# A linear-attention, soft-MoE and MLP kernel: r multiplies, diagonals and one bonus on other engines, w2 rows in long runs, one weight piece narrowed later

## The chip, the core and the metric

The kernel runs on one core of a Trainium2 chip. The metric is device time in microseconds, lower is better; three runs of the kernel before gave 387.38, 387.45 and 388.14 us. The core has TensorE (PE, matmuls), VectorE (DVE), ScalarE (ACT) and GpSimd (POOL), each of which works through its own instructions in the order in which they are written, and SyncE (SP), which issues the loads and stores here.

## The reference, cut

```
# attention: 4 batches, 8 heads, 768 positions, head width 48
for t in range(S):
    cur = einsum('bhd,bhe->bhde', u * k[t], v[t])
    y[t] = einsum('bhd,bhde->bhe', r[t], state + cur)
    state = w[:, :, None] * state + einsum('bhd,bhe->bhde', k[t], v[t])
x = y as 3072 tokens x 384
# first mlp: soft mixture, 8 experts x 4 slots, hidden 1024
logits = x @ phi
slot_input = softmax(logits over tokens).T @ x
slot_out[e] = relu(slot_input[e] @ w1[e]) @ w2[e]
x = softmax(logits over slots) @ slot_out
# second mlp: hidden 2048
h = x @ w_in
out = maximum(0.01 * h, h) @ w_out
```

All arrays are float32.

## The kernel before, in words

**Attention.** The sequence is cut into 6 chunks of 128 positions and the heads into 4 pairs: 24 units, unit i being chunk i // 4 and pair i % 4. The loop over i (line 572) is one turn; in turn i the engines work on units i - 1 to i + 4. For a unit j it runs: `load(j)` in turn j - 4 (rk is r and k by head row, tk is v, k and r by position); `scale(j)` in turn j - 2, which multiplies r and k (two multiplies, lines 305 to 310) by powers of the decay. The k one is always on DVE, the r one on POOL unless j is in `SCALE_V`. Then `bonus(j)` (POOL, lines 316 and 319: r times u, times k), `diag(j)` (DVE sums it into Dg, line 324, and base(j) is filled with the diagonals: eight ACT activations, line 339, or one POOL affine select, line 330, for units in `AFFINE`), and `keys(j)` (line 351, POOL, or DVE for units in `KEYS_V`), all in turn j - 2. In turn j - 1 come `scores(j)` (16 matmuls into A, line 362; the pool of A has one buffer) and `keep(j)` (two predicated copies on DVE from A into base, line 370). In turn j come `attend(j)` (lines 393 and 401, into Y), the copy of Y into xT (line 434), and `update(j)`, the state products U (line 415) and their addition to St on DVE (line 423). The powers of the decay for a head pair are made by `powers` on DVE and ACT, then transposed (line 297) and copied by ACT to KH (line 298), which `keys` multiplies by. U, the transposes psE and px and the tile `low` of the narrowing share a PSUM pool of two buffers. `FILL_L` puts two filling matmuls (line 584) in turn 2. In the second turn of each chunk (i % 4 = 1, "slot turn") the soft-max part of the chunk before is added: transposes, slot products (line 519), acc and sst on DVE (lines 530, 532); its maxima are taken in the turn before (lines 475 to 479).

The weights of both mlps arrive during this: list entry n of `WST` is the turn in which weight load n is issued on SP. The second mlp's weights come as 64-bit numbers and are narrowed to 32 bits: in the turns of `NARROW` three DVE instructions (lines 174, 180, 185) do half a piece, after an ACT instruction (line 170) in a turn of `NARROW_A`.

**First mlp.** `hidden(0)`, `hidden(1)` (line 755) make the slots' hidden values, `outer` (line 798) multiplies by w2: the first half of the experts from tiles loaded by `load_w2`, the second half from `load_rows(f)`, one tile for each of 8 blocks f. Loads of w_out (`load_wout(j)`, tiles wor) are issued among them. Two pieces of w_out are narrowed (`conv_a` on ACT, `conv_b`, `conv_c`, `conv_d` on DVE, lines 848 to 858) and split by `parts` into a high part (woh, ACT, line 864) and a low part (wol, POOL, line 865) around the last `outer`.

**Second mlp.** 96 steps over (token block, hidden block f): a matmul h (line 963), the leaky maximum (t, lines 969 and 973), split into gh and gl (lines 977, 982), and nine products o (line 1020). The products of step n and the preparation of step n + 3 are written in one turn, followed by the jobs listed for n: `job(n, fn, arg)` puts further narrowing there. Steps 4 and 5 are the first with f = 2.

Of the kernel before, what the change touches and what calls it, by code (L numbers as in the profile page):

```python
# [21 lines left out]
NU = NC * NP  # L22
DM = H * D
# [10 lines left out]
NLAST = 3  # L34
NLD = 5
NWT = 18
AFFINE = (0, 1)
KEYS_V = (4, 5, 6)
FILL = {0: 2, 1: 1}
FILL_L = {3: 2}  # L40
WST = [*range(2, 19), 20, 20, 21, 21, NU]
NARROW = [5, 7, 9, 11, 15, 19, 20, 22]
NARROW_A = {3: 5, 6: 7, 7: 9, 10: 11, 14: 15, 18: 19, 19: 20, 21: 22}
SCALE_V = (9, 13, 17, 21)
WCH = 8
WH = WCH // 2
WCW = 768
# [3 lines left out]


def body(
    tc, rk, tok, wT, urep, phi, w1, w2, win, wout, seq, uw, wT1, urep1, rk1, tok1, outT, dbg=None
):
    nc = tc.nc
    ok = chunked(tc, rk, tok, wT, urep, phi, w1, w2, win, wout, outT, dbg, True)


    with tc.If(ok != R * NP):  # L60
        rk2 = nc.dram_tensor("rk2", rk.shape, F32, kind="Internal").ap()
        tok2 = nc.dram_tensor("tok2", tok.shape, F32, kind="Internal").ap()
        general(tc, seq, uw, rk1, tok1, rk2, tok2)
        chunked(tc, rk2, tok2, wT1, urep1, phi, w1, w2, win, wout, outT)


@with_exitstack
# [49 lines left out]


@with_exitstack
def chunked(ctx, tc, rk, tok, wT, urep, phi, w1, w2, win, wout, outT, dbg=None, check=False):  # L120
    nc = tc.nc
    cp = ctx.enter_context(tc.tile_pool(name="cp", bufs=1))
    wp = ctx.enter_context(tc.tile_pool(name="wp", bufs=NWT))
# [220 lines left out]
    def keys(i, eng=nc.gpsimd):  # L344
        if i >= NU - NP:
            return
        hp = i % NP
        kk = tk_t[i][:, 1]
        if i in KEYS_V:
            eng = nc.vector  # L350
        eng.tensor_tensor(
            kk, kk, KH[:, hp : hp + 1, :].broadcast_to([128, B, 2 * D]), op=ALU.mult
        )
# [194 lines left out]

    def load_rows(f):
        t = wp.tile([128, 4, DM], F32, name=f"w2_{f}", tag="wt")  # L550
        nc.sync.dma_start(t, w2[4:, :, f].rearrange("e p d -> p e d"))
        for g in range(4):
            w2_sb[FT * (4 + g) + f] = t[:, g]

# [10 lines left out]
    keep(0)  # L565
    bonus(1, nc.vector)
    diag(1)
    keys(0)
    powers(2)
    powers(3)  # L570

    for i in range(NU):
        c, k = divmod(i, NP)
        for n in range(len(WST)):
            if WST[n] == i:
                load_weights(n)
        if i + NLD - 1 < NU:
            load(i + NLD - 1)
        else:
            load_w2_unit(i + NLD - 1 - NU)  # L580
        if i + 2 < NU:
            scale(i + 2)
        for _ in range(FILL_L.get(i + 1, 0)):
            nc.tensor.matmul(
                lw[0].rearrange("p a t -> p (a t)")[:, C:], ident,
                u_sb.rearrange("p a d -> p (a d)"), start=False, stop=True, skip_group_check=True,
            )
        if i + 1 < NU:
            scores(i + 1)
            keep(i + 1)  # L590
        slot = bool(c) and k == 1
        if i >= 1 and not slot:
            logits(i - 1)
        if 2 <= i < NP:
            tokens(i - 2)(nc.scalar.copy)
        if i + 2 < NU:
            bonus(i + 2, nc.gpsimd if i else nc.vector)
        attend(i)
        if slot:
            soft2(c - 1)  # L600
        evac(i)
        if c and k == 0:
            soft1(c - 1)
        if i < NP - 1:
            powers_t(i + 1)
            keys(i + 1)
        if i == NP:
            nc.gpsimd.memset(ones, 1.0)
        if i == NU - 2:
            yps[NU - 1] = psE.tile([128, 4, C], F32, name="ylast", tag="E")  # L610
            nc.vector.memset(yps[NU - 1][32:64, 0:2], 0.0)
        if check and i == NU - 2:
            rc0 = ap.tile([R, NP], F32, name="rc0")
            nc.vector.tensor_single_scalar(rc0, w_sb, WLO, op=ALU.is_ge)
            nc.vector.scalar_tensor_tensor(rc0, w_sb, WHI, rc0, op0=ALU.is_le, op1=ALU.mult)
            nc.vector.tensor_reduce(mst[:R, 6:7], rc0, op=ALU.add, axis=AX.X)
            nc.vector.memset(mst[:R, 7:8], 1.0)
        if i + 2 < NU:
            diag(i + 2)
            if i + 2 >= NP:  # L620
                keys(i + 2)
        update(i)
        if i >= NP - 1:
            tok_copy = tokens(i - 1)
        if slot:
            pS = slots(c - 1)
            logits(i - 1)
        if i >= NP - 1:
            tok_copy(nc.scalar.copy)
        if slot:  # L630
            slots_add(c - 1, pS)
        if i in NARROW:
            j, x = divmod(NARROW.index(i), 2)
            w = slice(x * WCW // 2, (x + 1) * WCW // 2)
            low = psM.tile([128, WCW // 2], I32, name=f"low{i}", tag="m")
            narrow_b(wirs[j], w, low)
            narrow_c(wi[:, j, w], wirs[j], w, low)
            narrow_d(wi[:, j, w], wirs[j], w, low)
        if i in NARROW_A:
            j, x = divmod(NARROW.index(NARROW_A[i]), 2)  # L640
            w = slice(x * WCW // 2, (x + 1) * WCW // 2)
            narrow_a(wi[:, j, w], wirs[j], w)
# [164 lines left out]
        load_wide(wout[j], wor[j])  # L807

    hs0 = hidden(0)
    for j in range(2):  # L810
        load_wout(j)
    for f in range(2, FT):
        load_rows(f)
    mix(0)
    hs1 = hidden(1, lambda: hidden_t(0, hs0))
    for j in range(2, WH):
# [48 lines left out]
        nc.gpsimd.tensor_tensor(l, w, a.bitcast(F32), op=ALU.subtract)  # L865

    conv_a(0)
    conv_a(1)
    outer(1, range(FT))
    for p in range(2):  # L870
        conv_b(p)
        conv_c(p)
        conv_d(p)
        parts(p)
    for j in range(WH, WCH):
        wirs[j] = wp.tile([128, WCW, 2], I32, name=f"wir{j}", tag="wt")
        load_wide(win[j], wirs[j])
# [183 lines left out]
        job(32 + q, lambda q: late.update({q: spread(1, (2 * q, 2 * q + 1), pH, "h")}), q)  # L1061
        job(32 + q, lambda q: late[q](nc.scalar.copy), q)

    for f in (2, 3):
        job(0, parts, f)

    hid_a(2)
    hid_b(2)
# [54 lines left out]
def _layout(i):  # L1123
    import numpy as np

    r, k, v = (np.asarray(i[n]) for n in ("r", "k", "v"))

    def pad(x):
        y = np.zeros(x.shape[:1] + (2, 64) + x.shape[3:], np.float32)
        y[:, :, :D] = x  # L1130
        return y.reshape(x.shape[:1] + (128,) + x.shape[3:])

    def rows(x):
        y = x.reshape(B, NP, 2, NC, C, D).transpose(3, 1, 2, 5, 0, 4)
# [12 lines left out]
    a["wT"] = wt.reshape(NP, 128)[:, :R].T
    a["urep"] = np.broadcast_to(np.asarray(i["u"]).reshape(NP, 2 * D), (128, NP, 2 * D))
    ph = np.zeros((NP, 2, 64, NS), np.float32)
    ph[:, :, :D] = np.asarray(i["moe_phi"]).reshape(NP, 2, D, NS)  # L1150
    ph = np.stack([ph, ph[:, ::-1]], 1).reshape(NP, 2, 128, NS)
    a["phi"] = ph[:, :, :R].transpose(2, 0, 1, 3)
    a["w1"] = np.asarray(i["moe_w1"]).reshape(E, KT, 128, 2, FE // 2).transpose(0, 3, 2, 1, 4)
    a["w2"] = np.asarray(i["moe_w2"]).reshape(E, FT, 128, DM).transpose(0, 2, 1, 3)
    wi, wo = np.asarray(i["moe2_w_in"]), np.asarray(i["moe2_w_out"])
    wi = wi.reshape(KT, 128, WCH, FF // WCH).transpose(2, 1, 0, 3).reshape(WCH, 128, WCW)
    wo = wo.reshape(WCH, 2, 128, DM).transpose(0, 2, 1, 3).reshape(WCH, 128, WCW)
    s = np.stack([np.asarray(i[n]).reshape(B * H, S, D) for n in "rkv"])
    w, u = (np.asarray(i[n]) for n in "wu")
    uw = np.broadcast_to(np.stack([u, w], 1), (16, H, 2, D)).reshape(128, 2, D)  # L1160

    one = np.zeros((3, D), np.float32)
    one[:, 0], one[:, 1] = (1.0, 0.5, 1.0), (1.0, -0.5, -1.0)
    rk1 = np.broadcast_to(one[:2].T[None, None, :, :, None, None], (1, 2, D, 2, B, C))
    rk1 = pad(rk1)[0]
    tok1 = np.broadcast_to(np.tile(one[1::-1], (1, 2 * B)), (128, 2, 2 * B * D))
    rest = {"win": None, "wout": None, "seq": s, "uw": uw}
    rest["wT1"] = np.ones((R, NP), np.float32)
    rest["urep1"] = np.broadcast_to(np.tile(one[2], 2), (128, NP, 2 * D))
    rest["rk1"], rest["tok1"] = rk1, tok1  # L1170
# [24 lines left out]
```

## Time and profile before

| | |
|---|---|
| median of three runs | 387.45 us |
| profiled execution, whole time | 386.47 us |
| its span, first to last instruction | 384.70 us |
| busy: PE, DVE, ACT, POOL | 367.6, 275.9, 233.3, 144.1 us |
| attention | 0 to about 118 us |
| first mlp | about 123 to 149 us |
| second mlp | about 156 to 380 us |
| DMA, until about 155 us | 16 engines busy nearly all the time, some 410 GB/s |

TensorE is granted full clock throughout (0.999 on average). A timeline row gives start, length, engine, line, operation, output and inputs, shapes, and in brackets how long the engine was idle before it and what ended that. The chain of waits that ended last goes through POOL's products between 22 and 45 us, through TensorE, DVE and ACT in turn from there to 118, and through TensorE's o products at the end.

### The profile page before, as it was taken

The numbers are of one execution on the slowest core, as the hardware profiler recorded it, in microseconds if no ns is written. First come the engines' busy times: TensorE is split into PE (matmuls) and PEld (weight loads), VectorE is DVE, ScalarE is ACT, GpSimd is POOL, SyncE is SP. The second block draws the span as 40 slices with busy tenths as digits, with TensorE's granted clock in tenths as the row PEclk, the third lists the DMA queues.
The fourth block names the chain that finished last, engine by engine and source line by source line (L and its number), as shares of the span: only waits on it lengthen the run. The fifth ranks groups of instructions, "written<-read, shape, count | busy, mean of one in ns | idle before, by whom it ended". The sixth has DMA issues, their size and how long they took to land.

```text
span 384.7 us, 8325 instructions
## 1 busy us (share of the span) xinstructions
PE 367.6 (96%) x3162; PEld 283.4 (74%) x3162; DVE 275.9 (72%) x478; ACT 233.3 (61%) x542; POOL 144.1 (37%) x144
## 2 busy tenths in 40 slices
PE   6889998999999999899999999999999999999994
PEld 3567777787875345788888878888888888888883
DVE  6978888888887448677577746777766766586762
ACT  3288797888894224766765657667655445545440
POOL 4779999977713103336333312554200000000000
PEclk9999999999999999999999999999999999999999
DMA  7999999999999999200022220000000220030202
GB/s 262 401 412 412 407 417 415 418 414 415 399 412 382 371 402 425 84 2 0 0 85 82 83 83 0 1 2 1 2 2 0 82 83 0 1 133 33 82 3 89
DMA packets 21090, 70.16 MB, mean 182 GB/s; under 512 B 2240, under 2 KB 7344, under 8 KB 20912
## 3 DMA queue, kind: packets, MB, share of 16 engines
q1 hardware_dynamic: 21040, 69.53, 46.0%
q8 instruction: 27, 0.44, 0.5%
q14 instruction: 23, 0.19, 0.1%
HBM read 64.80 MB, written 4.72 MB: 181 GB/s over the span
## 4 chain that ended last, share of the span: by engine, by line
PE 76%; DVE 8%; ACT 5%; POOL 5%; issue 2%; DMA 2%; SPq 1%; POOLq 0%; DVEq 0%; ACTq 0%
PE o L1020 51%; PE h L963 6%; ACT base L339 3%; PE po L798 3%; PE ph L755 3%; PE A L362 2%; PE Y L401 2%; DVE base L370 2%; DMA tk<-in_tok_dram 2%; POOL tk L316 1%; POOL rkb L310 1%; POOL tk L319 1%; PE Y L393 1%; PE px L451 1%; DVE Dg L324 1%
## 5 line engine op out<-in xcount | busy, mean ns | idle before, releaser
L977 ACT CAST gh<-t 128x512 fp32r<-128x512 f32 x94 | 58.5, 622 | 69.5 <-DVE t L973 66.6
L973 DVE TENSOR_TENSOR t<-t,h 128x512 f32<-128x512 f32 (+1 forms) x97 | 65.8, 679 | 25.3 <-ACT t L969 24.6
L1020 PE MATMUL o<-gh,wol 128*128 128x512 f32 x279 | 80.2, 393 | 0.0
L1020 PE MATMUL o<-gh,woh 128*128 128x512 f32 x279 | 80.0, 393 | 0.0
L1020 PE MATMUL o<-gl,woh 128*128 128x512 f32 x279 | 79.7, 392 | 0.0
L982 DVE TENSOR_TENSOR gl<-t,gh 128x512 fp32r<-128x512 f32 x71 | 50.2, 707 | 40.4 <-ACT gh L977 40.4
L969 ACT ACTIVATE t<-h 128x512 f32<-128x512 f32 (+1 forms) x97 | 57.4, 592 | 12.5 <-PE h L963 11.2
L1020 PEld LDWEIGHTS o<-gh,woh 128*128 128x128 f32 x279 | 52.4, 188 | 11.8 <-DVE sum L1091 0.2
L1020 PEld LDWEIGHTS o<-gl,woh 128*128 128x128 f32 x279 | 52.5, 188 | 11.7
L1020 PEld LDWEIGHTS o<-gh,wol 128*128 128x128 f32 x279 | 52.2, 188 | 11.7 <-issue 0.4
L339 ACT ACTIVATE base<-anti,Dg 128x128 f32<-128x128 f32 x176 | 53.9, 389 | 10.5 <-DVE Dg L324 9.7
L982 POOL TENSOR_TENSOR gl<-t,gh 128x512 fp32r<-128x512 f32 x23 | 34.3, 1491 | 51.0 <-ACT gh L977 43.6
L370 DVE COPY_PREDICATED base<-mask,A 128x512 f32<-128x512 int32 x48 | 34.2, 734 | 7.4 <-ACT base L339 6.7
L963 PE MATMUL h<-cT,Gs 128*128 128x512 f32 (+1 forms) x97 | 37.4, 391 | 1.4 <-ACT Gs L931 1.4
L362 PE MATMUL A<-rkb 48*128 48x128 f32 x384 | 28.5, 289 | 4.3 <-DVE base L370 2.1
L362 PEld LDWEIGHTS A<-rkb 48*128 48x128 f32 x384 | 24.2, 192 | 9.9 <-issue 3.3
L401 PE MATMUL Y<-base,tk 128*48 128x128 f32 x376 | 25.5, 277 | 0.0
L310 POOL TENSOR_TENSOR rkb<-rkb,ETw 112x512 f32<-112x512 f32 x19 | 23.4, 1234 | 1.9 <-DMA rkb<-in_rk_dram 1.9
L316 POOL TENSOR_TENSOR tk<-tk,u_sb 128x384 f32<-128x384 f32 x21 | 22.1, 1051 | 5.4 <-DMA tk<-in_tok_dram 3.5
L401 PEld LDWEIGHTS Y<-base,tk 128*48 128x48 f32 x376 | 19.4, 122 | 4.9 <-issue 4.3
L963 PEld LDWEIGHTS h<-cT,Gs 128*128 128x128 f32 x97 | 18.0, 188 | 5.6 <-ACT Gs L931 1.8
L865 POOL TENSOR_TENSOR wol<-wor,woh 128x384 fp32r<-128x384 f32 x8 | 9.5, 1198 | 33.3 <-ACT woh L864 33.3
(199 smaller groups left out, 484.0 us busy)
## 6 DMA issues: line engine op xcount, KB each, us to landing
w<-in_w_dram SPq DMA_DIRECT2D x24, 768.0 KB, 8.7
tk<-in_tok_dram SPq DMA_DIRECT2D x23, 576.0 KB, 7.0
rkb<-in_rk_dram SPq DMA_DIRECT2D x24, 512.0 KB, 7.4
wir<-in_win_dram SPq DMA_DIRECT2D x8, 768.0 KB, 11.3
out_dram<-sum SPq DMA_DIRECT2D x17, 256.0 KB, 2.1
wor<-in_wout_dram SPq DMA_DIRECT2D x4, 768.0 KB, 10.3
wir<-in_wout_dram SPq DMA_DIRECT2D x4, 768.0 KB, 4.3
w2t<-in_w_dram SPq DMA_DIRECT2D x4, 576.0 KB, 7.5
```

The source lines that it names most:

```text
L310: (nc.vector if x or i in SCALE_V else eng).tensor_tensor(t, t, e, op=ALU.mult)
L316: eng.tensor_tensor(rr, rr, u_sb[:, hp : hp + 1, :].broadcast_to([128, B, 2 * D]), op=ALU.mult)
L339: nc.scalar.activation(base[i][:, h, b, :], anti, AF.Copy, scale=Dg[i][:, h * B + b : h * B + b + 1])
L362: nc.tensor.matmul(a[:, h, b, :], rk_t[i][p0 : p0 + D, 1, b, :], rk_t[i][p0 : p0 + D, 0, b, :], start=True, stop=True,)
L370: nc.vector.copy_predicated(base[i][:, :, 2 * j : 2 * j + 2, :], mask.unsqueeze(1).unsqueeze(1).broadcast_to([128, 2, 2, C]), a[:, :, 2 * ...
L401: nc.tensor.matmul(ys[r][g : g + D, j, :], v[:, b, D * h : D * h + D], base[i][:, h, b, :], start=c == 0, stop=True, skip_group_check=True,)
L963: nc.tensor.matmul(t, Gs[f // 8][:, f % 8 * 128 : f % 8 * 128 + 128], cT[blk // 3][:, blk % 3 * TB + c.start : blk % 3 * TB + c.stop], sta ...
L969: nc.scalar.mul(tt[n][:, c], t, 0.01)
L973: nc.vector.tensor_tensor(tt[n][:, c], tt[n][:, c], h, op=ALU.max)
L977: nc.scalar.copy(gh[n][:, c], tt[n][:, c])
L982: eng.tensor_tensor(gl[n][:, c], tt[n][:, c], gh[n][:, c].bitcast(F32), op=ALU.subtract)
L1020: nc.tensor.matmul(os[m][:, c], w[j][:, k, m * 128 : (m + 1) * 128], g[n][:, c], start=k == 0 and w is woh and g is gh and c.start == 0, s ...
```

## The change

It renumbers the tables of the attention loop, moves a few calls, changes the memory layout of the second half of w2, and moves the narrowing of the second piece of w_out.

- The r multiply of units 3 to 6 and of every odd unit from 9 on goes to DVE (`SCALE_V`); before it was units 9, 13, 17 and 21. The diagonals of units 7, 11, 15, 19 and 23 go from ACT to a POOL affine select. The key products of units 4 to 6 go from DVE back to POOL, the bonus of unit 2 from DVE to POOL.
- `keys(0)`, `powers(3)` and `update(0)` come later in the first turns, and within a turn `keys(i + 2)` now stands before `diag(i + 2)`.
- Weight loads leave turns 8 and 14 and come two turns' worth later; the narrowings of turns 9, 11, 15 and 19 move to 8, 12, 16 and 18.
- The second half of w2 is stored so that a tile of `load_rows` is one run of 6144 bytes for a partition instead of four of 1536; the loads of w_out go behind two and behind all of these tiles.
- The second piece of w_out is narrowed and split in steps 0 to 3 of the second mlp.

```diff
-AFFINE = (0, 1)
-KEYS_V = (4, 5, 6)
+AFFINE = (0, 1, 7, 11, 15, 19, 23)
-WST = [*range(2, 19), 20, 20, 21, 21, NU]
-NARROW = [5, 7, 9, 11, 15, 19, 20, 22]
-NARROW_A = {3: 5, 6: 7, 7: 9, 10: 11, 14: 15, 18: 19, 19: 20, 21: 22}
-SCALE_V = (9, 13, 17, 21)
+WST = [*range(2, 8), *range(9, 14), *range(15, 19), 20, 20, 21, 21, 22, 22, NU]
+NARROW = [5, 7, 8, 12, 16, 18, 20, 22]
+NARROW_A = {3: 5, 6: 7, 7: 8, 11: 12, 15: 16, 17: 18, 19: 20, 21: 22}
+SCALE_V = (3, 4, 5, 6, 9, 11, 13, 15, 17, 19, 21, 23)
...
-        if i in KEYS_V:
-            eng = nc.vector
...
-        nc.sync.dma_start(t, w2[4:, :, f].rearrange("e p d -> p e d"))
+        nc.sync.dma_start(t, w2f[f])
...
-    keys(0)
     powers(2)
-    powers(3)
...
-            bonus(i + 2, nc.gpsimd if i else nc.vector)
+            bonus(i + 2)
+        if i == 0:
+            keys(0)
...
+        if i == 0:
+            powers(3)
...
         if i + 2 < NU:
-            diag(i + 2)
             if i + 2 >= NP:
                 keys(i + 2)
-        update(i)
+            diag(i + 2)
+        for u in {0: (), 1: (0, 1)}.get(i, (i,)):
+            update(u)
...
-    for j in range(2):
-        load_wout(j)
     for f in range(2, FT):
+        if f == 4:
+            load_wout(0)
         load_rows(f)
+    load_wout(1)
...
     conv_a(0)
-    conv_a(1)
     outer(1, range(FT))
-    for p in range(2):
-        conv_b(p)
-        conv_c(p)
-        conv_d(p)
-        parts(p)
+    conv_b(0)
+    conv_c(0)
+    conv_d(0)
+    for f in range(2):
+        parts(f)
...
-    for f in (2, 3):
-        job(0, parts, f)
+    job(0, conv_a, 1)
+    job(0, conv_b, 1)
+    job(1, conv_c, 1)
+    job(2, conv_d, 1)
+    job(2, parts, 2)
+    job(3, parts, 3)
```

POOL from the key product of unit 11 on, before: key product, r multiply of unit 12, its two bonus products, its key product, then unit 13 (tk_855 is the tile of unit 13, tk_776 of unit 12, rkb_111 holds r and k of unit 12).

```order
L351 TENSOR_TENSOR tk_701<-tk_701,KH 128x384
L310 TENSOR_TENSOR rkb_111<-rkb_111,ETw 112x512
L316 TENSOR_TENSOR tk_776<-tk_776,u_sb 128x384
L319 TENSOR_TENSOR tk_776<-tk_776 128x384
L351 TENSOR_TENSOR tk_776<-tk_776,KH 128x384
```

The same place now (base_894 and Dg_892 are unit 11's, tk_767 is unit 12's):

```order
L348 TENSOR_TENSOR tk_694<-tk_694,KH 128x384
L329 AFFINE_SELECT base_894<-Dg_892 128x1024
L309 TENSOR_TENSOR rkb_111<-rkb_111,ETw 112x512
L315 TENSOR_TENSOR tk_767<-tk_767,u_sb 128x384
L318 TENSOR_TENSOR tk_767<-tk_767 128x384
```

An affine select that reads Dg of unit 11, which DVE makes, now stands ahead of everything that POOL does for unit 12; in the other units of the chunk there is none.

DVE in turns 18 and 19 before, from the Dg of unit 20 to the keep of unit 20 (base_1604) and the Dg of unit 21:

```order
L324 TENSOR_REDUCE Dg_1602<-tk_1398 128x4x2
L423 SCALAR_TENSOR_TENSOR St<-St,W_139,U_1613 112x192
L310 TENSOR_TENSOR rkb_110<-rkb_110,ETp 112x512 x2
L370 COPY_PREDICATED base_1604<-mask,A_1635 128x2x256 x2
L324 TENSOR_REDUCE Dg_1670<-tk_1477 128x4x2
```

And now (base_1573 is unit 20's):

```order
L323 TENSOR_REDUCE Dg_1571<-tk_1369 128x4x2
L420 SCALAR_TENSOR_TENSOR St<-St,W_139,U_1582 112x192
L173 TENSOR_SCALAR low_1598<-wir_462 128x384
L179 SCALAR_TENSOR_TENSOR low_1598<-wi,low_1598 128x384
L184 SCALAR_TENSOR_TENSOR wi<-wir_462,low_1598 128x384
L309 TENSOR_TENSOR rkb_110<-rkb_110,ETp 112x512 x2
L367 COPY_PREDICATED base_1573<-mask,A_1607 128x2x256 x2
```

The three instructions of a narrowing have come in between the Dg and the keep of unit 20; before they stood one turn later, behind the Dg of unit 21.

ACT in steps 0 to 3 of the second mlp before (wor_2089 is the second piece of w_out, wor_2147 the third):

```order
L969 ACTIVATE t_2445<-h_2444 128x512
L864 CAST woh_2250<-wor_2089 128x384 x2
L977 CAST gh_2446<-t_2445 128x512
L969 ACTIVATE t_2479<-h_2478 128x512
L977 CAST gh_2480<-t_2479 128x512
L969 ACTIVATE t_2500<-h_2499 128x512
L848 ACTIVATE wfa<-wor_2147 128x768
L977 CAST gh_2501<-t_2500 128x512
```

And now (wor_2066 is the second piece):

```order
L969 ACTIVATE t_2406<-h_2405 128x512
L849 ACTIVATE wfa<-wor_2066 128x768
L977 CAST gh_2407<-t_2406 128x512
L969 ACTIVATE t_2438<-h_2437 128x512
L977 CAST gh_2439<-t_2438 128x512
L969 ACTIVATE t_2460<-h_2459 128x512
L849 ACTIVATE wfa<-wor_2112 128x768
L865 CAST woh_2215<-wor_2066 128x384
L977 CAST gh_2461<-t_2460 128x512
```

The copy of the second piece's first half (woh) moved from step 0 to step 2, behind the first narrowing instruction of the third piece.

## Rows read from the trace of the kernel before

**Rows 1.** Windows view, three stretches: length, PE, PEld, DVE, ACT, POOL busy, clock, DMA.

```profile
22.72:48.94 26.22, 25.34 (x444) 20.40 (x444) 22.23 (x42) 21.80 (x69) 25.41 (x26) 1.00 1.02 411
48.94:111.98 63.04, 60.38 (x1090) 48.40 (x1089) 55.09 (x108) 53.29 (x170) 48.90 (x47) 1.00 1.02 412
...
160.00:380.00 220.00, 219.36 (x984) 178.92 (x982) 149.73 (x221) 129.27 (x224) 48.78 (x37) 1.00 0.10 36
```

**Rows 2.** Timeline of PE: fill, then scores of units 3, 12, 15, 16, 23.

```profile
20.13 1.56 PE L584 MATMUL l<-u_sb,ident 128*128 128x384 f32 x4
22.72 1.16 PE L362 MATMUL A<-rkb 48*128 48x128 f32 x16 [1.03 <-DVE base L370]
...
63.52 1.16 PE L362 MATMUL A<-rkb 48*128 48x128 f32 x16 [1.05 <-DVE base L370]
...
77.13 1.16 PE L362 MATMUL A<-rkb 48*128 48x128 f32 x16
...
81.15 1.16 PE L362 MATMUL A<-rkb 48*128 48x128 f32 x16
...
111.98 1.16 PE L362 MATMUL A<-rkb 48*128 48x128 f32 x16
```

**Rows 3.** Timeline of POOL: affine select of unit 1, multiply and bonus of unit 12.

```profile
12.55 1.09 POOL L330 TENSOR_SCALAR_AFFINE_SELECT base<-Dg 128x1024 f32<-128x1024 f32 x1 [2.24 <-DVE Dg L324]
...
55.34 1.28 POOL L310 TENSOR_TENSOR rkb<-rkb,ETw 112x512 f32<-112x512 f32 x1
56.58 1.01 POOL L316 TENSOR_TENSOR tk<-tk,u_sb 128x384 f32<-128x384 f32 x1
57.66 1.00 POOL L319 TENSOR_TENSOR tk<-tk 128x384 f32<-128x384 f32 x1
```

**Rows 4.** Timeline of ACT: base of unit 2, KH of pair 2.

```profile
19.26 2.45 ACT L339 ACTIVATE base<-anti,Dg 128x128 f32<-128x128 f32 x8 [3.92 <-DVE Dg L324]
...
22.08 0.23 ACT L298 COPY KH<-psE 128x96 f32<-128x96 f32 x1
```

**Rows 5.** Timeline of DVE, turns 7 and 8: multiplies, keep, narrowing, Dg, next multiply.

```profile
45.33 1.27 DVE L310 TENSOR_TENSOR rkb<-rkb,ETp 112x512 f32<-112x512 f32 x2
46.53 0.72 DVE L370 COPY_PREDICATED base<-mask,A 128x512 f32<-128x512 int32 x1
...
49.14 0.56 DVE L174 TENSOR_SCALAR low<-wir 128x384 int32<-128x384 uint32 x1
...
50.87 0.68 DVE L310 TENSOR_TENSOR rkb<-rkb,ETp 112x512 f32<-112x512 f32 x1
51.47 1.36 DVE L370 COPY_PREDICATED base<-mask,A 128x512 f32<-128x512 int32 x2
...
53.23 0.55 DVE L324 TENSOR_REDUCE Dg<-tk 128x8 f32<-128x384 f32 x1
...
54.01 0.68 DVE L310 TENSOR_TENSOR rkb<-rkb,ETp 112x512 f32<-112x512 f32 x1
```

**Rows 6.** One line's view, the loads of w2 rows (L551): waiters, landing times.

```profile
  PEld po L798: 0.3, 1
...
DMA to landing us min/median/max: 6.9/10.8/12.5
```

**Rows 7.** Timelines in and before steps 2 to 6 of the second mlp.

```profile
146.53 0.96 DVE L185 SCALAR_TENSOR_TENSOR wor<-wor 128x768 int32<-128x768 int32 x1
...
163.66 0.60 ACT L969 ACTIVATE t<-h 128x512 f32<-128x512 f32 x1 [0.48 <-PE o L1020]
...
165.76 0.85 PE L1020 MATMUL o<-gh,woh 128*128 128x512 f32 x3
...
170.93 1.46 DVE L185 SCALAR_TENSOR_TENSOR wor<-wor 128x768 int32<-128x768 int32 x1
...
172.42 0.55 ACT L864 CAST woh<-wor 128x384 fp32r<-128x384 f32 x1 [0.20 <-DVE wor L185]
...
173.04 1.04 POOL L865 TENSOR_TENSOR wol<-wor,woh 128x384 fp32r<-128x384 f32 x1 [1.47 <-ACT woh L864]
```

More of the change, by code (lines that the diff above doesn't have):

```diff
@@ L53, in body @@
 def body(
-    tc, rk, tok, wT, urep, phi, w1, w2, win, wout, seq, uw, wT1, urep1, rk1, tok1, outT, dbg=None
+    tc, rk, tok, wT, urep, phi, w1, w2, w2f, win, wout, seq, uw, wT1, urep1, rk1, tok1, outT, dbg=None
 ):
     nc = tc.nc
-    ok = chunked(tc, rk, tok, wT, urep, phi, w1, w2, win, wout, outT, dbg, True)
+    ok = chunked(tc, rk, tok, wT, urep, phi, w1, w2, w2f, win, wout, outT, dbg, True)
     with tc.If(ok != R * NP):
@@ L63, in body @@
         general(tc, seq, uw, rk1, tok1, rk2, tok2)
-        chunked(tc, rk2, tok2, wT1, urep1, phi, w1, w2, win, wout, outT)
+        chunked(tc, rk2, tok2, wT1, urep1, phi, w1, w2, w2f, win, wout, outT)
 @with_exitstack
@@ L119, in chunked @@
 @with_exitstack
-def chunked(ctx, tc, rk, tok, wT, urep, phi, w1, w2, win, wout, outT, dbg=None, check=False):
+def chunked(ctx, tc, rk, tok, wT, urep, phi, w1, w2, w2f, win, wout, outT, dbg=None, check=False):
     nc = tc.nc
@@ L1153, in _layout @@
     a["w1"] = np.asarray(i["moe_w1"]).reshape(E, KT, 128, 2, FE // 2).transpose(0, 3, 2, 1, 4)
-    a["w2"] = np.asarray(i["moe_w2"]).reshape(E, FT, 128, DM).transpose(0, 2, 1, 3)
+    w2 = np.asarray(i["moe_w2"]).reshape(E, FT, 128, DM)
+    a["w2"], a["w2f"] = w2[: E // 2].transpose(0, 2, 1, 3), w2[E // 2 :].transpose(1, 2, 0, 3)
     wi, wo = np.asarray(i["moe2_w_in"]), np.asarray(i["moe2_w_out"])
```

## The prediction

> **What bounds the kernel now.** I read the busy shares by stage first, then each engine's timeline around the steps that the diff touches. In the second mlp (160 to 380 us) TensorE is idle for 0.64 of 220 us [rows 1]: nothing there can be gained, and any stall is paid in full. In the attention TensorE is idle for 0.88 us between 22.72 and 48.94 and for 2.66 us from there to 111.98 [rows 1]. So moving work off POOL, ACT and DVE can gain 3.5 us there at most, plus what the first turns hold. It can lose more, because beside TensorE runs a second loop of nearly the same length, and that loop decides this case. Call a unit j one pair of heads in one chunk. Its diagonal goes: bonus(j), two POOL products; Dg(j), a DVE sum; base(j), eight ACT copies (or one affine select on POOL); keep(j), two masked DVE copies from the scores A(j). There is one A tile, so A(j+1) on TensorE waits for keep(j). TensorE's own turn is 4.02 us (A(15) to A(16) [rows 2]). Dg 0.55, base 2.45 and the second half of keep 0.75, which follow one another because Dg(j+1) stands behind keep(j) on DVE, take 3.75 us. Anything over a quarter us that gets between them shows on TensorE.
>
> **The first turns.** The bonus of unit 2 goes from DVE to POOL. After the affine select of unit 1, which ends at 13.64 [rows 3], POOL takes the r multiply (1.05 from start to start), then two products of 1.08 and 1.00: bonus(2) ends at 16.75. Dg(2) 0.55, base(2) 2.45 and two hand-offs of 0.05 to 0.1 end base(2) at 19.9, where it now ends at 21.71 (19.26 + 2.45 [rows 4]). That looks like 1.8 us won, but the state products of unit 0 were moved into turn 1 as well. With two buffers in that PSUM pool, the products of unit 1 now wait for the buffer that the key copy KH(2) empties, and on ACT KH(2) stands behind base(2) and the copy of Y: it ends 0.60 after base(2) (22.08 + 0.23 against 21.71 [rows 4]), at 20.6. Then 0.6 for the products and 1.56 for the fill matmuls [rows 2], and A(3) starts at 22.7, as before (22.72 [rows 2]). Gain 0; if POOL's products are stretched by 0.4 the loss is that, and if the fill hides it all, 1.0 is gained.
>
> From A(3) to A(9) POOL sheds four multiplies of 1.24 (units 3 to 6, to DVE), takes three key products of 1.00 from DVE, and base(7) leaves ACT for POOL. Bonus 5 and 6 come 0.5 to 0.9 earlier, and I take 0.66 of the 0.88 us idle as won. Bounds 0 and 0.88.
>
> **Units 8 to 23, the sum.** Three edits meet here: r of every odd unit now takes two DVE multiplies (1.20 where one of 0.68 was [rows 5]); every fourth diagonal (11, 15, 19, 23) is an affine select on POOL; a narrowing of weights (1.73 on DVE, 49.14 to 50.87 [rows 5]) stands at the end of turns 8, 12, 16, 18, 20 and no longer 9, 11, 15, 19. The 1.05 us that TensorE waited at 63.52 for keep(11) [rows 2] was behind the narrowing of turn 9: that is won.
>
> What is lost: DVE after keep(9) (start 51.47) reaches Dg(10) at 53.23 and is free at 54.01 [rows 5]; now 1.73 of narrowing, 1.20 of multiplies and 1.36 of keep(10) follow: 58.30, less the 0.66 won: 57.65. So A(11) starts at 57.9 and Dg(11) ends at 58.1.
>
> POOL then runs in order: the affine select of unit 11 waits for Dg(11), and behind it stand the r multiply and the bonus of unit 12, which used to be done long before. From the end of Dg(11): 0.1, affine 1.05, multiply 1.24, products 1.08 and 1.00 [rows 3], so bonus(12) ends 4.47 later; Dg(12) 0.55, base(12) 2.45, half a keep 0.75 [rows 4, 5] and four hand-offs of 0.1: A(13) can start 8.62 after it, at 66.7. TensorE would be ready at 57.9 + 2 turns of 4.02 and a little = 66.0: a new wait of 0.7. The loop goes on: keep(12) ends at 8.4, unit 13 takes 3.75, the soft-max rows 0.4, Dg(14) and the state 0.85, the narrowing 1.73, two multiplies 1.20, keep(14) 1.26, Dg(15) 0.55: 18.14 from Dg(11) to Dg(15). TensorE needs about 17.4 for the same four turns. So Dg(15) ends at 76.2 and Dg(19) at 94.4.
>
> After Dg(19) it is worse, since the narrowing of turn 18 stands on DVE behind Dg(20), and Dg(20) waits for the late bonus(20): 4.57, Dg and state 0.83, narrowing 1.73, multiplies 1.20, keep(20) 1.36, hand-off 0.26: A(21) starts 9.96 after Dg(19), at 104.3, and TensorE waits 2.1 us. Unit 21 takes 3.75, then 0.4, Dg(22) 0.47, narrowing 1.73, multiplies 1.20, keep 1.36, 0.26: A(23) at 113.2, against 111.98 [rows 2]. The attention ends **1.24 us later**. Each figure of the loop is from a row, but the sum is of small differences: I give it 2.9 us of gain (no POOL wait binds) to 2.0 of loss (the first turns lose 0.4 and the waits add up).
>
> **The first mlp.** Rows of w2 are read in longer runs and ahead of the second piece of output weights. TensorE waited 0.3 us in all for these rows before, and they landed 6.9 to 12.5 us after issue [rows 6]; TensorE comes 1.2 us later now, so the loads keep their cover: 0. If the cover were gone TensorE would wait in its 64 outer matmuls; the bound is the 0.3 it shows. Narrowing the second piece leaves DVE before the output copy, where DVE is not waited for: 0, between 0 and 0.3 of gain.
>
> **The second mlp.** The second piece is now narrowed in steps 0 to 2 and copied in steps 2 and 3. Its first copy is wanted by the first product of step 4, at 165.76 [rows 7]. The last narrowing instruction stands on DVE behind the max of hidden block 5. That block's ACT copy t ends at 164.26 now and may end half a us sooner, since POOL has no low parts to make ahead of it; with the max of 0.7 after it this is about 164.6. The narrowing step takes 0.96 [rows 7], the ACT copy 0.55, so the weights are there at 166.2; POOL's low part takes 1.04 more and costs another 0.15. Stall 0.6, bounds 0 and 1.1.
>
> Sum: 1.24 + 0.6 = 1.8 us. The profiled execution took 386.47 us (span 384.70), so its counterpart takes 388.3; the median of the runs is 387.45, 0.98 above it, and the same sum on it gives 389.3.
>
> **Rivals.** (1) The change does as meant: POOL keeps its lead, neither affine select nor the narrowing of turn 18 delays keep. It decides if POOL reaches the bonus of the unit after the affine within 3.7 us of Dg, 0.8 less than I add up. Then the 2.66 and 0.66 us idle go, less about 0.6 of copies on ACT that remain, and 0.6 is lost in the second mlp: 2.1 us faster, 385.4. For it: TensorE is then the only bound. Against it: POOL's queue order, in which the wait for Dg stands ahead of the next unit's work. 0.2.
>
> (2) The affine waits cost their 0.7, but bonus(20) comes in time, so turn 18 costs no 2.1: A(21) at 102.9, A(23) at 111.8, attention 0.2 faster, second mlp 0.6 slower: 387.9, no change. 0.2.
>
> (3) Port lock. The narrowing's last step, the same instruction, took 0.96 at 146.53 and 1.46 at 170.93, where POOL worked beside it [rows 7]. If the moved one takes 1.46 the stall is 1.1 and the time 389.8. The Trainium skill's page "SBUF — State Buffer", section "Who interferes with whom", says that a DVE instruction with two SBUF inputs and a GpSimd instruction that reads SBUF hold their shared port exclusively, one blocking the other; by that rule, the two rows agree, and it speaks against moving narrowing beside POOL's work. 0.1.
>
> **How the numbers follow.** The forecast has 0.5, with its own range 388.4 to 390.4. About 0.2% (0.77 us) is what a measurement of this kernel can tell from no change. Slower is the forecast and rival 3: 0.6; no change is rival 2: 0.2; faster is rival 1: 0.2. The range cuts half of rival 1 and the upper end of the forecast: 385.6 to 390.6.
>
> **What would show it.** Right: A(3) near 22.7; POOL idle before each L330 affine select of units 11, 15, 19, released by Dg; Dg(12), (16), (20) on DVE released by POOL's L319; TensorE waiting some 2 us for keep(20), near 104; a gap of about half a us in the o products near step 4, ended by ACT's woh. Wrong: turns of 4.02 us throughout from A(8) to A(23), an A(23) well before 112, or a new wait of the outer matmuls for rows of w2. What would make the prediction wrong most easily is the first part: if A(3) or bonus(8) comes 1 us earlier or later, all units behind it do.

## The result, and the profile after

The changed kernel took 392.3 us (median of 390.18, 391.71, 392.89 and 393.47), the kernel before 387.56 in the same series: a ratio of 1.0114, 95% interval 1.0066 to 1.0161. In a later series on one chip (`again` below) it took 390.28 against 387.14, ratio 1.0088 (1.0065 to 1.0111). It is slower, as forecast, and by more: forecast were 389.3 us and a range of 385.6 to 390.6, which holds the 390.28 of the later series but not the 392.3. The profiled execution took 391.71 us (span 389.7) where 388.3 was forecast; before it was 386.47 (384.7).

The windows of the changed kernel, with the columns of [rows 1] (length, PE, PEld, DVE, ACT and POOL busy, granted clock, DMA):

```profile
22.40:48.09 25.69, 25.21 (x445) 20.36 (x444) 20.47 (x39) 18.32 (x57) 22.02 (x24) 1.00 1.01 410
48.09:115.06 66.97, 62.66 (x1090) 49.73 (x1089) 57.78 (x112) 46.06 (x146) 48.73 (x49) 0.97 0.99 392
104.00:106.00 2.00, 0.79 (x13) 0.61 (x12) 2.00 (x6) 0.24 (x2) 1.72 (x3) 1.00 0.98 387
...
108.00:110.00 2.00, 2.00 (x18) 1.57 (x14) 1.69 (x6) 1.61 (x5) 0.00 (x0) 0.50 0.98 389
110.00:112.00 2.00, 2.00 (x30) 1.68 (x32) 1.86 (x4) 2.00 (x10) 0.00 (x0) 0.75 1.04 433
160.00:380.00 220.00, 219.72 (x981) 178.08 (x980) 152.42 (x223) 132.07 (x229) 48.91 (x37) 1.00 0.09 33
```

From A(9) (48.09) to A(23) (115.06) it is 66.97 us, where [rows 1] had 63.04, and TensorE idles 4.31 instead of 2.66; the rest is counted as busy, part of it at a lower clock (`again`, at full clock there, has 61.21 busy for 62.66). Behind 106 the granted clock is at half (1.2 GHz) for a while, right after a stretch in which TensorE was busy for 0.79 of 2 us. The starts of the scores, to be read against [rows 2] (A(3), A(11), A(12), A(13), A(15), A(19), A(21), A(22), A(23)):

```profile
22.40 1.16 PE L359 MATMUL A<-rkb 48*128 48x128 f32 x16
...
58.31 1.16 PE L359 MATMUL A<-rkb 48*128 48x128 f32 x16 [0.15 <-PE l L440]
62.56 1.16 PE L359 MATMUL A<-rkb 48*128 48x128 f32 x16
67.20 1.16 PE L359 MATMUL A<-rkb 48*128 48x128 f32 x16
...
76.78 1.16 PE L359 MATMUL A<-rkb 48*128 48x128 f32 x16 [0.15 <-PE l L440]
...
95.24 1.16 PE L359 MATMUL A<-rkb 48*128 48x128 f32 x16
...
105.42 1.16 PE L359 MATMUL A<-rkb 48*128 48x128 f32 x16 [1.21 <-issue]
...
110.20 1.52 PE L359 MATMUL A<-rkb 48*128 48x128 f32 x16
...
115.06 1.16 PE L359 MATMUL A<-rkb 48*128 48x128 f32 x16
```

The forecast had 22.7 for A(3), 57.9 for A(11), 66.7 for A(13), 104.3 for A(21) and 113.2 for A(23). TensorE loses 1.9 us in turn 20 (A(21) comes 5.93 behind A(20), where a turn takes 4.02), and 2.1 were forecast. The attention ends 3.08 us later (115.06 against 111.98), the first hidden matmul comes 11.42 us behind A(23) in both kernels, the first matmul h of the second mlp 30.1 us behind that in both, so the first mlp cost nothing. The remaining 1.9 us were lost in the second mlp.

The wait that the forecast rested on, around units 11 and 12 on DVE and POOL (the affine rows answer to [rows 3], Dg to [rows 5]):

```profile
58.11 0.53 DVE L323 TENSOR_REDUCE Dg<-tk 128x8 f32<-128x384 f32 x1
...
58.80 1.09 POOL L329 TENSOR_SCALAR_AFFINE_SELECT base<-Dg 128x1024 f32<-128x1024 f32 x1 [3.54 <-DVE Dg L323]
...
59.86 1.28 POOL L309 TENSOR_TENSOR rkb<-rkb,ETw 112x512 f32<-112x512 f32 x1
...
62.18 1.00 POOL L318 TENSOR_TENSOR tk<-tk 128x384 f32<-128x384 f32 x1
...
63.21 0.56 DVE L323 TENSOR_REDUCE Dg<-tk 128x8 f32<-128x384 f32 x1 [1.44 <-POOL tk L318]
```

POOL stood idle for 3.54 us for Dg(11), then did unit 12's multiply and bonus, and DVE stood idle for 1.44 us for that. Dg(16) and Dg(20) show the same 1.43 and 1.44.

### The profile page after: what moved, and what is told of

The parts are those of the page before. It is cut to its first block, busy times and chain, and to the rows that moved or that the text cites. A ratio compares the mean times of both kernels' runs of the same rounds, so it can differ in the third digit from the quotient of the medians.

```text
span 389.7 us, 8263 instructions
## 1 busy us (share of the span) xinstructions
PE 371.0 (95%) x3162; PEld 284.6 (73%) x3162; DVE 276.1 (71%) x481; ACT 221.4 (57%) x502; POOL 141.8 (36%) x146
## 4 chain that ended last, share of the span: by engine, by line
PE 69%; DVE 12%; POOL 8%; ACT 5%; issue 4%; POOLq 0%; DVEq 0%; ACTq 0%
PE o L1020 49%; PE h L963 5%; ACT base L338 4%; PE po L798 3%; PE ph L755 3%; DVE base L367 2%; DVE Dg L323 2%; POOL tk L318 2%; POOL tk L315 2%; DVE rkb L309 2%; PE Y L398 1%; POOL tk L348 1%; POOL base L329 1%; POOL rkb L309 1%; PE A L359 1%
## 5 line engine op out<-in xcount | busy, mean ns | idle before, releaser
L338 ACT ACTIVATE base<-anti,Dg 128x128 f32<-128x128 f32 x136 | 41.6, 390 | 11.0 <-DVE Dg L323 11.0
L398 PE MATMUL Y<-base,tk 128*48 128x128 f32 x376 | 26.3, 283 | 0.0
L309 DVE TENSOR_TENSOR rkb<-rkb,ETp 112x512 f32<-112x512 f32 x35 | 22.8, 680 | 0.9 <-DMA rkb<-in_rk_dram 0.5
L318 POOL TENSOR_TENSOR tk<-tk 128x384 f32<-128x384 f32 x22 | 22.1, 1005 | 1.7
L431 ACT COPY xT<-Y 112x512 f32<-112x512 f32 x23 | 13.4, 582 | 15.8 <-PE Y L398 15.8
```

What stands on the lines that cost most here:

```text
L309: (nc.vector if x or i in SCALE_V else eng).tensor_tensor(t, t, e, op=ALU.mult)
L338: nc.scalar.activation(base[i][:, h, b, :], anti, AF.Copy, scale=Dg[i][:, h * B + b : h * B + b + 1])
L398: nc.tensor.matmul(ys[r][g : g + D, j, :], v[:, b, D * h : D * h + D], base[i][:, h, b, :], start=c == 0, stop=True, skip_group_check=True,)
```

## What the experiments showed

### The two halves apart

`attn_only` is the changed kernel with the output weights loaded, and their second piece narrowed, where they were before; `mlp_only` makes the opposite edit in the kernel before. Part of the edit of `attn_only`:

```diff
-        if f == 4:
-            load_wout(0)
+    for j in range(2):
+        load_wout(j)
...
-    job(0, conv_a, 1)
...
-    job(3, parts, 3)
+    for f in (2, 3):
+        job(0, parts, f)
```

> The attention of the changed kernel (and w2 in long runs), but the second piece of output weights loaded and narrowed where it was before. Theory: attention and second mlp add up. A(23) near 115.1 as in the changed kernel (114.3 if the clock does not fall), no wait in step 4 of the second mlp and steps of 2.29 us there again, so the span is 384.7 + 3.1 = 387.8 (387.0 without the fall). Rival: the slower steps of the second mlp (2.31 us instead of 2.29) come from the attention or the layout of w2; then they stay and the span is about 388.9.

> The kernel before with two edits only: loads of w_out behind two and behind all of the w2 tiles (w2 itself laid out as before), and the second piece narrowed in steps 0 to 3 of the second mlp. Theory: attention as before (A(23) at 112.0), a stall of 0.8 us at step 4, and the steps behind it 2.31 us instead of 2.29 because they follow a stall: 1.9 us in all, span 386.6, a ratio of 1.005. Rival: the slow steps do not belong to this edit: 0.8 us, span 385.5, ratio 1.002.

`attn_only` took 390.01 us, ratio 1.0081 (1.0062 to 1.0100), span 387.2, A(23) at 113.92, no wait in steps 4 and 5. `mlp_only` took 389.23, ratio 1.0057 (1.0038 to 1.0076), span 387.2, with steps 4 and 5 at 2.86 and 2.47 us instead of 2.29: 0.75 us lost there, as in the changed kernel (0.77). Both halves lose; the two ratios overlap, so these runs do not tell which loses more. But two thirds of `mlp_only`'s profiled loss (1.57 of 2.5 us) lie in its attention, which is that of the kernel before: its clock was at half there.

```profile
18.00:20.00 2.00, 2.00 (x23) 1.39 (x22) 1.97 (x4) 0.15 (x1) 2.00 (x2) 0.50 1.03 411
...
22.00:24.00 2.00, 2.00 (x19) 1.54 (x19) 1.67 (x4) 1.37 (x6) 1.03 (x2) 0.50 0.97 398
```

These windows of `mlp_only` show the fall, which lasts from about 17 to 24 us; A(3) came at 25.01 instead of 22.72, and A(23) at 113.55 instead of 111.98. The wait of TensorE ahead of it (1.31 us, for a POOL product) is just as long in the kernel before, whose clock stayed. So a fall behind such a wait happens in some executions and not in others.

### Diagonals back on ACT

```diff
-AFFINE = (0, 1, 7, 11, 15, 19, 23)
+AFFINE = (0, 1, 7)
```

> The changed kernel with the diagonals of units 11, 15, 19 and 23 back on ACT (unit 7 stays on POOL). Theory: POOL's wait for Dg ahead of the next unit's bonus is what makes four turns take 18.5 us; without it they take 17.5, as in the kernel before between A(13) and A(17) (17.6): A(9) 48.1, A(21) 100.8, no idle of DVE before Dg(12), (16), (20), A(23) near 109.7, the clock does not fall, second mlp 0.8 to 1.8 later by its stall: span 383 to 384. Rival: ACT, with four more bases of 2.45 us, binds in the turns with soft-max rows and four turns stay above 18 us: A(23) above 111.5, span above 385.5.

`act_diag` took 387.55 us, ratio 1.0012 (0.9994 to 1.0030): this edit alone takes back what the changed kernel lost. DVE no longer waits for Dg(12); it follows keep(11) at once, as its rows say:

```profile
61.42 0.75 DVE L367 COPY_PREDICATED base<-mask,A 128x512 f32<-128x512 int32 x1 [0.34 <-ACT base L338]
62.07 0.53 DVE L323 TENSOR_REDUCE Dg<-tk 128x8 f32<-128x384 f32 x1
```

From A(13) to A(17) it takes 17.38 us (forecast 17.5), against 18.46 in the changed kernel; A(23) comes at 111.12. That is later than the 109.7 expected: 0.7 was lost at unit 10, where the running maximum (see below) took 0.69 us instead of 0.15, and 0.5 at A(21), where DVE ran without a pause from Dg(20) through the narrowing of turn 18 to keep(20). DVE waited for ACT at neither place, so the rival (ACT binds) is not the cause. The first hidden matmul now comes 11.84 behind A(23): base(23) on ACT costs 0.42 there, which POOL's affine select had saved. Span 386.0, of which the second mlp's loss is 1.56.

### The narrowing of turn 18

```diff
-NARROW = [5, 7, 8, 12, 16, 18, 20, 22]
-NARROW_A = {3: 5, 6: 7, 7: 8, 11: 12, 15: 16, 17: 18, 19: 20, 21: 22}
+NARROW = [5, 7, 8, 12, 16, 19, 20, 22]
+NARROW_A = {3: 5, 6: 7, 7: 8, 11: 12, 15: 16, 18: 19, 19: 20, 21: 22}
```

> The changed kernel with the narrowing of turn 18 back in turn 19 (its ACT step in 18). Theory: its 1.8 us on DVE between Dg(20) and keep(20) go, A(21) at 103.6 instead of 105.4; in turn 19 the narrowing lies beside base(21) on ACT (2.45), so A(22) and A(23) keep most of it, the clock does not fall: A(23) at 112.5 and a span near 387.1. Rival: the wait only moves to unit 21, since narrowing and multiplies (3.0 us) together are longer than base(21): A(23) above 113.5, span above 388.

Turn 20 of the changed kernel, on DVE, is what the forecast had written out row by row:

```profile
100.15 0.55 DVE L323 TENSOR_REDUCE Dg<-tk 128x8 f32<-128x384 f32 x1 [1.44 <-POOL tk L318]
...
101.06 0.56 DVE L173 TENSOR_SCALAR low<-wir 128x384 int32<-128x384 uint32 x1
...
102.80 1.28 DVE L309 TENSOR_TENSOR rkb<-rkb,ETp 112x512 f32<-112x512 f32 x2
103.99 1.33 DVE L367 COPY_PREDICATED base<-mask,A 128x512 f32<-128x512 int32 x2
```

From the end of Dg(19) (95.57) to A(21) it took 9.85 us; the forecast had 9.96. With the narrowing one turn later (`n19`), A(21) comes 4.65 behind A(20) instead of 5.93, but A(22) now waits:

```profile
103.67 1.16 PE L359 MATMUL A<-rkb 48*128 48x128 f32 x16
108.21 1.16 PE L359 MATMUL A<-rkb 48*128 48x128 f32 x16 [0.89 <-DVE st L472]
```

From A(21) to A(22) it is 4.54 us where `fill20` (below), without a fallen clock, has 3.87. Of 1.28 us gained, 0.67 were given back: both theories were half right. The time was 389.31, ratio 1.0067, span 386.6.

### The running maximum

The soft-max rows keep a running maximum of 128 numbers, one instruction of one column. In this profile of the changed kernel it took 0.82 us at unit 10 and 0.55 at unit 14, each time while POOL did a product:

```profile
52.10 1.00 POOL L315 TENSOR_TENSOR tk<-tk,u_sb 128x384 f32<-128x384 f32 x1 [0.31 <-DMA tk<-in_tok_dram]
...
52.30 0.82 DVE L476 TENSOR_TENSOR mst<-mst,st 128x1 f32<-128x1 f32 x1
...
71.05 0.55 DVE L476 TENSOR_TENSOR mst<-mst,st 128x1 f32<-128x1 f32 x1
```

The kernel before has such rows too. There it took 0.15 at unit 10, between two POOL products, but 0.35 at unit 14 and, at unit 18:

```profile
89.22 0.83 DVE L479 TENSOR_TENSOR mst<-mst,st 128x1 f32<-128x1 f32 x1
```

In these three rows the maximum ends within 0.03 us of the POOL product beside it (53.10, 71.57 and 90.04). Whether a product lies there at unit 10 differs between executions: POOL's product waits for its tk tile to be loaded, and in `again` it starts only at 53.46, after the maximum. The same line there:

```profile
L476 DVE TENSOR_TENSOR mst<-mst,st x5: 149/150/538, 52.6 to 121.2; 128x1 f32<-128x1 f32 x5
```

`mst_fill` is `fill20` (below) with this edit:

```diff
-            nc.vector.tensor_tensor(mst[:, c : c + 1], mst[:, c - 1 : c], st[:, 0:1], op=ALU.max)
+            nc.vector.tensor_scalar(
+                mst[:, c : c + 1], st[:, 0:1], mst[:, c - 1 : c], 1.0, op0=ALU.max, op1=ALU.mult
+            )
```

> As fill20, with the running maximum of 128 numbers on DVE (0.55 to 0.82 us in three chunks, 0.15 alone) written as a tensor-scalar instruction with one tensor input. Theory: it waited for POOL's product beside it; in the new form it takes 0.2, A(11) comes 0.65 earlier than in fill20 (57.8 instead of 58.5), A(15) and A(19) 0.4 more each: A(23) near 113.1 instead of 114.4, time 1.3 us less than fill20. Rival: its length comes from elsewhere (its inputs) and stays, or what stands behind it waits as long: no change.

The line's own view of `mst_fill`, and its scores of units 11, 15 and 19:

```profile
L476 DVE TENSOR_SCALAR mst<-st,mst x5: 203/204/205, 52.4 to 120.4; 128x1 f32<-128x1 f32 x5
```

```profile
57.79 1.16 PE L359 MATMUL A<-rkb 48*128 48x128 f32 x16
...
75.93 1.16 PE L359 MATMUL A<-rkb 48*128 48x128 f32 x16
...
94.08 1.16 PE L359 MATMUL A<-rkb 48*128 48x128 f32 x16
```

All five now take 0.20 us, those of units 14 and 18 in the middle of a POOL product. The loop takes 18.14 and 18.15 us for four turns, against 18.47 and 18.46 in `fill20` and 18.45 to 18.48 in all seven profiles that share this loop and have the old form; the forecast's sum was 18.14. From A(3) to A(23) it gains 1.22 us on the profile of `fill20` (1.3 expected), but 0.62 of that was ahead of A(11), and that part is not shown to be the new form's: POOL stood idle at unit 10 in `mst_fill`, and `again`, `attn_only`, `n19` and `fill2`, with the old form at 0.15 there, come from A(3) to A(11) just as fast (35.25 to 35.27 us against 35.31). Against `again`, `fill20_b` and `fill2` the gain is 0.5 to 0.7. The median is 389.28, 0.6 under `fill20`, which two series do not tell apart; its clock fell in the first turns and its last steps were slow (below). The Trainium skill's page "SBUF — State Buffer", section "Who interferes with whom", has it that a DVE instruction with at most one SBUF input, outside the modes in which it uses both of its ports, does not contend with GpSimd, and that one with two does while GpSimd reads SBUF; by that rule, 0.20 beside a product and 0.82 and 0.55 in the old form agree.

### The clock behind the wait for keep(20)

`fill20` puts one more pair of filling matmuls ahead of A(21), `fill2` two more in turn 1 besides.

```diff
-FILL_L = {3: 2}
+FILL_L = {3: 2, 21: 1}
```

> The changed kernel with one more pair of filling matmuls (0.8 us of TensorE) in turn 20, ahead of A(21), where TensorE has been idle for 1.2 us. Theory: TensorE's granted clock falls to half between 107 and 111 us because TensorE idled before; filled, it stays at 1.00 there, A(21) stays at 105.4, A(23) comes 0.75 us earlier (114.3), the median is 1 to 2 us below 392.3 and the runs lie closer together. Rival: the fall has another cause; then the windows still show 0.5 near 108 and the time is 392 or more.

```profile
104.23 0.82 PE L579 MATMUL l<-u_sb,ident 128*128 128x384 f32 x2
105.62 1.16 PE L359 MATMUL A<-rkb 48*128 48x128 f32 x16 [0.56 <-issue]
...
114.44 1.16 PE L359 MATMUL A<-rkb 48*128 48x128 f32 x16
```

```profile
108.00:110.00 2.00, 1.78 (x26) 1.41 (x24) 1.54 (x6) 2.00 (x7) 0.11 (x1) 1.00 1.02 410
```

The clock stayed at full, and from A(21) to A(23) it took 8.82 us instead of 9.64: where it happens, the fall costs 0.82. The median was 389.88, which made it look as if the fall were worth 2.4, but the 392.3 is of another series. So both were run again, side by side.

> The changed kernel once more, in the same series as fill20_b and fill2. Theory: about 2 us of its loss are TensorE's granted clock at half behind the wait for keep(20), in most executions: median 391 to 392.5, spread over 2 us, profile with 0.5 somewhere between 105 and 115. Rival: the difference to fill20 was that between two series: median near 390.

> The changed kernel with 0.8 us of filling matmuls ahead of A(21), again. Theory: median 389.5 to 390, 1.5 to 2.5 under again, spread near 1.3 (the pace of the second mlp). Rival: as again.

> fill20 with two filling matmuls more in turn 1. Theory: the fall near 17 us is hidden in this order by the state products that wait for KH(2) (mst_fill: A(3) at 22.5 with it, best2 22.6), so nothing is gained: within 0.3 of fill20_b. Rival: part of fill20's executions lose there: 0.5 lower, and closer runs.

`again` took 390.28 (389.59 to 391.81), `fill20_b` 389.58 (389.13 to 392.05), `fill2` 390.0 (389.34 to 392.05): no difference that these runs can tell, and the rival was right. In `again` the clock did not fall at keep(20) at all, but at 17:

```profile
18.00:20.00 2.00, 2.00 (x22) 1.43 (x20) 1.42 (x3) 2.00 (x8) 1.92 (x3) 0.50 0.93 367
...
108.00:110.00 2.00, 1.80 (x28) 1.42 (x24) 1.97 (x6) 2.00 (x8) 0.00 (x0) 1.00 1.05 426
```

There it cost nothing: A(3) came at 22.69, and at 22.71 in `act_diag`, whose clock stayed, since the state products wait for KH(2) anyway. A(23) was at 113.87 and the span 388.2. `attn_only`, which has the same wait ahead of A(21) and no filling there, kept its clock too, so the full clock of `fill20` does not show that the filling kept it. What made the first series 2 us longer than this one is not settled. Its four executions had mean granted clocks of 0.984, 0.988, 0.993 and 0.998 at 393.47, 392.89, 391.71 and 390.18 us, which would fit more or longer falls, but only the one at 0.993 has a trace, and in `again` an execution at 0.988 took 390.70.

### The second piece of weights, one step earlier

```diff
-    job(1, conv_c, 1)
-    job(2, conv_d, 1)
-    job(2, parts, 2)
-    job(3, parts, 3)
+    job(0, conv_c, 1)
+    job(1, conv_d, 1)
+    job(1, parts, 2)
+    job(2, parts, 3)
```

> As act_diag, and the second piece of output weights narrowed one step earlier (second narrowing instruction in step 0, third in step 1, copies in steps 1 and 2). Its load lands near 149, so nothing else holds it. Theory: the 0.77 us that TensorE stalls in steps 4 and 5 of the second mlp go, and the steps behind it stay at 2.29 us instead of 2.31: 0.8 to 1.2 us less than act_diag. Rival: the narrowing on DVE now delays the max of steps 3 and 4, and TensorE waits for gh there as long: same time as act_diag.

The rival was right: 387.7 us against 387.55 of `act_diag`, and a stall of 0.69 in place of 0.75. DVE and TensorE there:

```profile
162.11 1.45 DVE L184 SCALAR_TENSOR_TENSOR wor<-wor 128x768 int32<-128x768 int32 x1
...
165.72 0.68 DVE L973 TENSOR_TENSOR t<-t,h 128x512 f32<-128x512 f32 x1
```

```profile
166.44 0.50 PE L963 MATMUL h<-cT,Gs 128*128 128x512 f32 x1 [0.37 <-DVE t L973]
```

The last narrowing instruction ran beside POOL's product (160.79 to 162.75) and took 1.45 instead of 0.95, and the maximum of the block behind it came late. In the changed kernel it took 0.95 and the copies were late:

```profile
167.72 0.95 DVE L184 SCALAR_TENSOR_TENSOR wor<-wor 128x768 int32<-128x768 int32 x1
...
168.71 0.53 ACT L865 CAST woh<-wor 128x384 fp32r<-128x384 f32 x1 [1.12 <-DVE wor L184]
...
169.29 0.96 PE L1020 MATMUL o<-gh,woh 128*128 128x512 f32 x3 [0.28 <-ACT woh L865]
...
170.40 0.53 PEld L1020 LDWEIGHTS o<-gh,wol 128*128 128x128 f32 x3 [0.35 <-POOL wol L866]
```

### What is best of both

`act_attn` joins the attention of `act_diag` to the second mlp of the kernel before. `best2` has the affine select for units 7 and 23 and the running maximum in its new form besides, `best3` two filling matmuls in turn 1, and `mlp_f1` is `mlp_only` with those.

> As act_diag, but the second piece of output weights loaded ahead of the w2 rows and narrowed before the second mlp, as in the kernel before. Theory: the loads, which run without a break, decide here: the last row of w2 lands near 148 as before while TensorE is 2 us earlier, so its 64 outer matmuls wait 1.5 to 2 us for rows of w2; no stall in step 4; span 384.0 to 384.5. Rival: the rows come earlier with the attention: no wait, span 382.5.

> The changed kernel with the second piece of output weights loaded and narrowed as before, diagonals of units 11, 15 and 19 on ACT, those of 7 and 23 on POOL, and the running maximum as a tensor-scalar instruction. Theory: as act_attn, and base(23) on POOL (1.1 us instead of 2.45, nothing behind it on POOL) gives back the 0.4 between A(23) and the first hidden matmuls; the maximum gives 0.5 at unit 22. A(23) 110.5, first hidden matmul 11.4 behind it, span 383.5, ratio 0.995. Rival: waits for loads take these gains (POOL waited 1.0 us for rk of unit 22 in act_attn): ratio 0.997 as act_attn.

> As best2, with two filling matmuls (0.56 us of TensorE) in turn 1 ahead of A(2), where TensorE idles 1.2 to 1.7 us. Theory: the clock fell near 17 us in some profiles (attn_only, mlp_only, mst_fill) and not in others (act_diag, n19) with the same wait there; filled, it does not fall, and where it falls in part of the runs of best2, the median is 0.3 to 0.5 lower and the runs lie closer. Rival: in these kernels the fall is hidden by the wait of the state products for KH that follows (attn_only: A(3) at 22.7 with the fall, 22.7 in act_diag without): same time as best2.

> mlp_only with the two filling matmuls in turn 1. In mlp_only the clock was half from 17 to 24 us and A(3) came 2.3 us later than in the kernel before, whose attention it shares. Theory: filled, the clock stays, A(3) is back near 22.7 to 23.0, and what is left of the 2.0 us that mlp_only lost is the stall and the pace in the second mlp, 0.7 to 1.0: median near 388. Rival: its median lies where it does for the second mlp alone: stays at 389.2.

`act_attn` took 386.62 us, ratio 0.9973 (0.9952 to 0.9994), A(23) at 111.26. The expected wait for rows of w2 did not come (0.2 us for this line, 0.3 in [rows 6]): the last tile of these rows was issued at 132.5 instead of 135.7, and the first hidden matmul, 11.83 behind A(23), came only 0.3 earlier than before. `best2` took 385.0, ratio **0.9943** (0.9923 to 0.9964), which beats both kernels by more than their noise: A(23) at 110.08, the first hidden matmul 11.42 behind it, span 383.7. `best3` took 385.93 (0.9945 to 0.9981): no gain from the filling, though its clock stayed and that of `best2` fell at 17. In `mlp_f1` the clock stayed and A(3) came at 22.84, as expected; it took 388.68, ratio 1.0024 (1.0009 to 1.0040): this half alone costs 1.2 us, with a profiled loss of 1.85 in the second mlp. What each of the three edits of `best2` is worth was not taken apart.

## Why the prediction was wrong

- **The direction, and the place: right.** POOL waits for Dg ahead of the next unit's work, DVE then waits for POOL, and the narrowing of turn 18 sits behind that. `act_diag` takes the loss back with one table. Rivals 1 and 2 are out: DVE waited 1.44 us for the bonus of units 12, 16 and 20.
- **The first turns: right.** The state products of unit 1 waited 1.31 us for KH(2), and A(3) came at 22.40 to 22.69 in the two profiles (22.7 forecast). A(9) came at 48.09 and 48.39 (48.28).
- **The step that failed: the loop of units 8 to 23, in its term "the soft-max rows 0.4".** It was read at unit 10 in [rows 5], where the maximum took 0.15 us; the 0.35 and 0.83 of the same trace, beside POOL's products, found no place in the sum. In the changed kernel these rows took 0.8, and Dg(15) and Dg(19) came 0.33 later each (18.47 and 18.46 for 18.14). All seven profiles with the old form agree, and `mst_fill` gives 18.14 and 18.15, so the term is shown to be the one. At unit 10 it is a matter of the execution: in this profile the rows took 1.0 and Dg(11) came 0.5 later than forecast, while in `again` A(11) came at 57.95 (57.9 forecast). A lock between DVE and POOL was in the prediction as rival 3, but for the narrowing in the second mlp, where it did not strike (0.95 us; in `act_jobs` it did, 1.45).
- **A term that was missing: the clock.** The profile before showed full clock throughout, and the sum had no price for a wait on TensorE beyond its length. Behind the 1.21 us ahead of A(21) it fell in one of the three profiles that have this wait (not in `again` and `attn_only`) and cost 0.82.
- **The second mlp: mechanism right, size short.** The stall was 0.77 (0.6 forecast, 0 to 1.1). The rest of the 1.9 is mostly the pace of the steps behind it (below), 1.05 in this profile, and that is not shown to belong to the edit. From the fourth to the 96th matmul h it takes 213.27 us on average in the eleven profiles with the narrowing there, 212.41 in the five without. Of these 0.86 the steps behind the stall hold 0.1, while single profiles of the eleven differ by 1.5 there; the rest is the stall.
- **The first mlp: right,** 0.2 us of waits for rows of w2, 0.3 before.
- **The range** had the stall's and the loop's bounds, but neither the clock nor the spread between executions. In the profiled execution the missing 3.2 us are 1.2 at Dg(19) (0.65 by the loop's term, the rest at unit 10), 0.8 of clock and 1.3 of stall and pace, less 0.1 in turn 20. Without a fall that costs anything, `again` is 3.5 over the kernel before in span, against 1.8 forecast: 1.9 by A(23) (1.24 forecast) and 1.6 in the second mlp (0.6 forecast). The 2 us between the medians of the two series stay open.

## What to carry to other kernels

An instruction that waits must not stand ahead of the next unit's independent work on the same engine: moving 1.1 us of diagonal to an engine with room cost a us per chunk because of what stood behind it. The same move was worth 0.4 us for the last unit, which has nothing behind it. When an engine's work is shifted in time, price the instructions of its neighbour again by what runs beside them, down to one-column ones, and write tiny ones with one tensor input where that can be done.

## What the runs showed that was not expected

**The pace of identical steps.** The steps of the second mlp hold the same ten matmuls each, at full clock, and yet take 2.29 or 2.315 us (30 steps at the start) and 2.28, 2.30 or 2.31 (43 at the end). TensorE's matmul h near the end, of the kernel before, of `n19` and of the changed kernel:

```profile
366.06 0.39 PE L963 MATMUL h<-cT,Gs 128*128 128x512 f32 x1
368.36 0.39 PE L963 MATMUL h<-cT,Gs 128*128 128x512 f32 x1
```

```profile
367.97 0.39 PE L963 MATMUL h<-cT,Gs 128*128 128x512 f32 x1
370.25 0.39 PE L963 MATMUL h<-cT,Gs 128*128 128x512 f32 x1
```

```profile
370.96 0.40 PE L963 MATMUL h<-cT,Gs 128*128 128x512 f32 x1
373.27 0.40 PE L963 MATMUL h<-cT,Gs 128*128 128x512 f32 x1
```

The pace changes almost only at a step with a wait or an odd length, and stays until the next. `n19`, `fill20`, `again` and the changed kernel share this part of the program and end at 2.28, 2.28, 2.30 and 2.31, so it is drawn in each execution: 0.03 us in each of 43 steps is 1.3 us. It fits that the ten times of `mlp_f1` fall into two groups, 387.4 to 387.7 and 388.6 to 389.2. What sets it was not found.
